# Splitting four V pages of a two-layer decode kernel into transfers of uneven row counts

## The chip, the core and the metric

The kernel runs on one core of a Trainium2 chip. The core has five engines with separate instruction streams: TensorE (PE) for matrix products, VectorE (DVE), ScalarE (ACT), GpSimd (POOL) and SyncE (SP), which here does nothing but issue transfers (DMAs) from the chip's main memory (HBM) to the on-chip memory of 128 partitions. The transfers are carried out by 16 DMA engines that work in parallel. The metric is the device time of one execution in microseconds (us). The kernel before takes 526.69 us, the median of two runs (526.36 and 527.03).

## The reference

Two layers, each of them an attention block and a gated feed-forward block, are applied to a single token of width 640. Both layers use the same weights and the same cache of keys and values.

```python
def _A_ref(x, k_cache, v_cache, wq, wo):      # Hq = Hkv = 32 heads, Dh = 192, Sk = 32768
    W = min(4096, max(256, Sk // 4))          # 4096: only the last 4096 positions count
    q = (x @ wq).reshape(B, Sq, Hq, Dh)       # (transposed to heads first)
    k = k_cache[:, :, Sk - W:, :]
    v = v_cache[:, :, Sk - W:, :]
    p = softmax(einsum("bhqd,bhkd->bhqk", q, k) * Dh ** -0.5)
    return einsum("bhqk,bhkd->bhqd", p, v).reshape(B, Sq, Hq * Dh) @ wo

def _B_ref(x, w1, w3, w2):                    # width 640 -> 1536 -> 640
    return (silu(x @ w1) * (x @ w3)) @ w2

x = x + _A_ref(layernorm(x), ...);  x = x + _B_ref(layernorm(x), ...)   # layer 0
x = x + _A_ref(layernorm(x), ...);  x = x + _B_ref(layernorm(x), ...)   # layer 1
```

One head's keys of the window are 4096 x 192 numbers of two bytes, 1.5 MB, and so are its values. For 32 heads and two layers that is most of what the kernel has to read.

## The kernel before

**Pages.** The keys or the values of one head are a page: 128 partitions x 6144 elements (`PGW`), that is 128 rows of 12,288 bytes, one row to a partition. The pages lie in one large tile, `arena`, of 32 units (`NUNIT`) of half a page each. Sixteen pages fit at once. The weights (wq, wo, w1, w3, w2) pass through the same units in pieces.

**The list of loads.** Before any work is recorded, a loop over the layers (lines 192 to 235) fills the list `loads`. An entry is a key, the number of units, and a list of parts; a part is an offset within the page's row, a width and a source in HBM. A whole page has one part:

```python
src = cache[0, h, S0:SK, :].rearrange("(p t) d -> p (t d)", p=P)
...
    loads.append(((kind, layer, h), 2, [(0, PGW, src)]))
```

In layer 0 the entries are: wq in three pieces, then K pages and V pages alternately, with V running `LEAD` = 6 heads behind K, then wo and the feed-forward weights. Layer 1 reads V again, and K for the heads that were not kept in `arena` from layer 0 (`RETAIN`).

**Issue.** `refill` takes the head of the list as long as `place` finds free units for it, and records one transfer on SP's queue for each part:

```python
for off, w, src in parts:
    pin(nc.sync.dma_start(out=arena[:, s * U + off:s * U + off + w], in_=src))
```

`done` frees a page's units after its last use and calls `refill`. So the order of the transfers is that of the list, and a transfer waits until whatever used its units before is done. There is a second wait, which the program's own list of waits shows: the completion of transfers is counted on eight semaphores in turn, and each transfer waits until the one eight places before it has landed completely. At most eight transfers are under way at a time. SP works strictly in order.

**Use of a page.** `k_page` (line 379 and the matrix products behind it) turns a K page by two DVE transposes and multiplies it with the queries; `softmax_head` and `softmax_place` turn four heads' scores into weights; `v_page` multiplies them with a V page, which must have landed whole. All matrix products are recorded by the helper `mm` (line 86). `combine`, `wo_proj` and `ffn` end a layer.

Of the kernel before, what the change touches and what calls it, by code (L numbers as in the profile page):

```python
# [15 lines left out]
P = 128  # L16
# [9 lines left out]
PGW = 6144  # L26
# [3 lines left out]
U = PGW // 2  # L30
# [8 lines left out]
MW = 2 * HB  # L39
PW = MW * HB  # L40
SPLIT = (("k", 12),)
KW = 4 * HB
WH = 6 * KW + 32 - KW
KEEP = 2400
# [3 lines left out]
def _ap(t, p0, npart, off, dims):  # L48
    ps = t.ap[0][0]
    return bass.AP(t.tensor, t.offset + p0 * ps + off, [[ps, npart]] + [list(d) for d in dims])  # L50
# [3 lines left out]
def kernel(  # L54
# [13 lines left out]
    nc = tc.nc  # L68
# [12 lines left out]
    def pin(ins):  # L81
        tc.keep_in_program_order(ins)
        return ins

    def mm(*a, **k):
        return pin(nc.tensor.matmul(*a, **k))  # L86
# [58 lines left out]
    arena = arn.tile([P, NUNIT * U], BF16, name="arena")  # L145
# [7 lines left out]
    loads = []  # L153
# [9 lines left out]
    def head(layer, g):  # L163
        return HG * ORDER[layer][g // HG] + g % HG

    def k_head(layer, g):
        return HG * ORDER[1][0] + (0, 1, 2, 3, 6, 4, 5, 7)[g] if layer == 1 and g < HG else head(layer, g)

    def k_first(layer, i):
        return layer == 0 and H - HB <= i < H  # L170

    def wo_units(layer):
        if layer == 0:
            return [(("o", 0, 0), [(1, 0, 2880)]), (("o", 0, 1), [(1, 2880, 5760)]), (None, [(0, 0, 5120), (1, 6720, 7680)]),
                    (("o", 0, 2), [(1, 5760, 6720), (2, 0, 1920)]), (("o", 0, 3), [(2, 1920, 4800)]),
                    (("o", 0, 4), [(2, 4800, 7680)]), (("o", 0, 5), [(3, 0, 2880)]), (("o", 0, 6), [(3, 2880, 5760)]),
                    (("o", 0, 7), [(3, 5760, 7680)]), (None, [(0, 5120, 7680)])]
        return [(("o", 1, 0), [(0, 0, 7680)]), (("o", 1, 1), [(1, 0, 7680)]), (("o", 1, 2), [(2, 0, 6720)])]
# [4 lines left out]
    def q_pieces(layer):  # L183
        if layer == 0:
            at = (0, 12, 24, 60)
            return [tuple(range(a, b)) for a, b in zip(at, at[1:])]
        return [tuple(range(12 * c + 6 * f, 12 * c + 6 * f + 6)) for f in range(2) for c in range(NCH)]

    def units_of(width):
        return -(-width // U)  # L190

    for layer in range(2):
        for piece in q_pieces(layer):
            n, at = 512 * len(piece), 512 * piece[0]
            loads.append((("q", layer, piece[0]), units_of(n), [(0, n, wq_r[:, at:at + n])]))
        for i in range(H + LEAD):
            kinds = (("v", i - LEAD, A_v_cache), ("k", i, A_k_cache))
            for kind, g, cache in kinds[::-1] if k_first(layer, i) else kinds:
                if not 0 <= g < H:
                    continue  # L200
                h = k_head(layer, g) if kind == "k" else head(layer, g)
                if kind == "k" and layer == 1 and h in RETAIN:
                    if h == STASH:
                        loads.append((("k", 1, h), 2, []))
                    continue
                src = cache[0, h, S0:SK, :].rearrange("(p t) d -> p (t d)", p=P)
                if layer == 1 and (kind, h) in SPLIT:
                    for th in range(2):
                        loads.append(((kind, layer, h, th), 1, [(0, U, src[:, U * th:U * th + U])]))
                else:  # L210
                    loads.append(((kind, layer, h), 2, [(0, PGW, src)]))
        for key, ranges in wo_units(layer):
            at, parts = 0, []
            for pos, lo, hi in ranges:
                parts.append((at, hi - lo, wo_v[ORDER[layer][pos]][:, lo:hi]))
                at += hi - lo
            if key:
                loads.append((key, units_of(at), parts))
            else:
                dst = wo5 if at == 2560 else wo4  # L220
                loads.append((None, None if dst is wo5 else LAST, [(dst[:, o:o + n], src) for o, n, src in parts]))
        if layer == 0:
            loads.append((("fa", layer), 1, [(0, 3072, w1_v[:, 0:3072])]))
            loads.append((("fb", layer), 1, [(0, 3072, w1_v[:, 3072:6144])]))
            loads.append((("fc", layer), 1, [(0, 1536, w1_v[:, 6144:]), (1536, 1536, w3_v[:, 0:1536])]))
            loads.append((("fd", layer), 1, [(0, 3072, w3_v[:, 1536:4608])]))
            loads.append((("fe", layer), 1, [(0, 3072, w3_v[:, 4608:])]))
            loads.append((("fg", layer), 1, [(0, W2A, w2_v[:, 0:W2A])]))
            loads.append((("fh", layer), 1, [(0, 7680 - KEEP - W2A, w2_v[:, W2A:7680 - KEEP])]))
            loads.append((None, None, [(keep[:], w2_v[:, 7680 - KEEP:7680])]))  # L230
        else:
            loads.append((("fa", layer), units_of(7680), [(0, 7680, w1_v[:, 0:7680])]))
            loads.append((("fb", layer), 2, [(0, PGW, w3_v[:, 0:PGW])]))
            loads.append((("fc", layer), 1, [(0, 1536, w3_v[:, PGW:])]))
            loads.append((("fd", layer), 2, [(o, n, w2_v[:, o:o + n]) for o, n in ((0, 3200), (3200, 1280), (4480, 3200 - KEEP))]))

    def place(key, n):
        at = [s for s in free if all(s + i in free for i in range(n))]
        if n == 2:
            at = [s for s in at if s % 2 == 0] or at  # L240
        kind, layer, x = (key + (None,))[:3]
        if layer == 0 and kind == "k" and x in RETAIN and x != STASH:
            return min((s for s in at if s < LAST), default=None)
        if layer == 0 and kind == "o":
            at = [s for s in at if s < LAST]
        if n == 1:
            return min(at, key=lambda s: (s ^ 1) in free, default=None)
        return max(at, default=None)

    def refill():  # L250
        while loads:
            key, n, parts = loads[0]
            if key is None:
                if n is not None:
                    if n not in free or n + 1 not in free:
                        return
                    free.remove(n)
                    free.remove(n + 1)
                for dst, src in parts:
                    pin(nc.sync.dma_start(out=dst, in_=src))  # L260
                loads.pop(0)
                continue
            s = place(key, n)
            if s is None:
                return
            home[key] = list(range(s, s + n))
            for i in home[key]:
                free.remove(i)
            loads.pop(0)
            for off, w, src in parts:  # L270
                pin(nc.sync.dma_start(out=arena[:, s * U + off:s * U + off + w], in_=src))  # L271
            if not parts:
                stash(arena[:, s * U:s * U + PGW], False)

    def stash(x, save):
        xu, pu, ru = x.bitcast(U32), pss[:].bitcast(U32), rest[:].bitcast(U32)
        at = 0
        for t, lo, n in [(pu, 512 * k, 512) for k in range(5)] + [(pu, MB + MN, 512 - MN), (ru, 0, MN)]:
            a, p = xu[:, at:at + n], t[:, lo:lo + n]
            pin(nc.vector.tensor_copy(out=p if save else a, in_=a if save else p))  # L280
            at += n
# [76 lines left out]
    def build_w(layer, b, first):  # L358
        engs = (nc.gpsimd, nc.scalar) + ((nc.vector, nc.vector) if first else (nc.gpsimd, nc.scalar))
        for a in range(4):  # L360
            dst = _ap(wst[:], 32 * a, 32, KW // 4 * a + HB - 1, [[WH - 1, HB], [KW, 6]])
            src = _ap(qt_sb[:], 0 if first else 32 * a, 32, 6 * HB * b, [[6, HB], [1, 6]])
# [18 lines left out]
    def k_page(layer, g, s_ps):  # L381
# [4 lines left out]
        for n in range(6):  # L386
            it = 5 - n
            be, par = divmod(it, 2)
            first = g % HB == 0 and n == 0
            w = 32 if first else KW  # L390
            for th in range(2):
                mm(s_ps[32 * th:32 * th + w, :], lhsT=wst[:, hl, KW * it:KW * it + w],
                   rhs=_ap(half(key, th), 0, P, 64 * be + par, [[192, 16], [2, 32]]),
# [7 lines left out]
    def softmax_head(b, s_ps):  # L401
# [7 lines left out]
        mb = _ap(m8[:], 0, 32, 0, [[0, 4], [1, HB]])  # L409
        pin(nc.vector.tensor_scalar_mul(out=tb[0:32, 0:KW].rearrange("p (a z) -> p a z", a=4), in0=mb, scalar1=-SCALE))  # L410
        pin(nc.scalar.mul(out=tb[32:64, 0:KW].rearrange("p (a z) -> p a z", a=4), in_=mb, mul=-SCALE))  # L411
        pin(nc.vector.transpose(nbt[:], tb[:]))  # L412
# [278 lines left out]
```

## Time and profile before

| what | value |
|---|---|
| median of two runs | 526.69 us |
| the profiled execution's own time | 525.68 us |
| its span | 523.7 us |
| PE, DVE, ACT, POOL busy | 286.0, 255.8, 66.0, 19.1 us |
| bytes moved by DMA | 220.12 MB, 420 GB/s over the span |
| transfers of whole K and V pages | 49 + 64, 1536 KB each |

The profile is a record of one execution. "Busy" is the time in which an engine worked on an instruction; for the DMA engines the share is a mean over all 16. The chain of waits is followed back from the last instruction: at each step it names what the instruction waited for last. A wait of SP's queue (SPq) says what a transfer waited for before it was issued. The record also holds each single packet that a DMA engine moved, with its size and duration but without the number of its engine, and for each transfer the marks that its engines set when their shares have landed.

### The profile page before, as it was taken

The numbers are of one execution on the slowest core, as the hardware profiler recorded it, in microseconds if no ns is written. First come the engines' busy times: TensorE is split into PE (matmuls) and PEld (weight loads), VectorE is DVE, ScalarE is ACT, GpSimd is POOL, SyncE is SP. The second block draws the span as 40 slices with busy tenths as digits, with TensorE's granted clock in tenths as the row PEclk, the third lists the DMA queues.
The fourth block names the chain that finished last, engine by engine and source line by source line (L and its number), as shares of the span: only waits on it lengthen the run. The fifth ranks groups of instructions, "written<-read, shape, count | busy, mean of one in ns | idle before, by whom it ended". The sixth has DMA issues, their size and how long they took to land.

```text
span 523.7 us, 5996 instructions
## 1 busy us (share of the span) xinstructions
PE 286.0 (55%) x2396; PEld 111.3 (21%) x2396; DVE 255.8 (49%) x385; ACT 66.0 (13%) x202; POOL 19.1 (4%) x86
## 2 busy tenths in 40 slices
PE   3335555463655544655555685676356565365564
PEld 1101222121222111212112231232112222122132
DVE  0079885656746476763002117431678565565002
ACT  1010210110202020202001022121201120112000
POOL 4010000000000000000000001000000000001000
PEclk9967778675776768666555577788557867776567
DMA  9999999999999999999999999999999999999996
GB/s 376 406 432 428 428 431 428 429 429 429 429 430 428 431 429 427 430 429 429 424 420 403 388 412 433 428 426 431 426 432 430 426 432 426 431 431 427 431 428 251
DMA packets 22931, 220.12 MB, mean 420 GB/s; under 512 B 2680, under 2 KB 3064, under 8 KB 7288
## 3 DMA queue, kind: packets, MB, share of 16 engines
q1 hardware_dynamic: 22760, 219.75, 99.2%
q8 instruction: 19, 0.31, 0.2%
q14 instruction: 8, 0.07, 0.0%
q10 hardware_dynamic: 144, 0.00, 0.0%
HBM read 219.74 MB, written 0.00 MB: 420 GB/s over the span
## 4 chain that ended last, share of the span: by engine, by line
DMA 84%; PE 10%; DVE 3%; issue 1%; ACT 1%; SPq 1%; DVEq 0%; ACTq 0%
DMA arena<-in_A_k_cache_dram 47%; DMA arena<-in_A_v_cache_dram 24%; DMA arena<-in_B_w_dram 6%; PE s_ps L86 5%; PE o_ps L86 2%; DVE arena L379 2%; DMA arena<-in_A_wo_dram 2%; DMA keep<-in_B_w_dram 2%; DMA arena<-in_A_wq_dram 1%; DMA wo<-in_A_wo_dram 1%; PE q_ps L86 1%; PE pss L86 1%; SPq L271 1%; PE u_ps L86 0%; PE y_ps L86 0%
## 5 line engine op out<-in xcount | busy, mean ns | idle before, releaser
L86 PE MATMUL s_ps<-arena,wst 128*16 128x512 bf16 (+1 forms) x768 | 157.7, 524 | 157.4 <-DVE arena L379 80.7
L379 DVE STREAM_TRANSPOSE arena<-arena 128x1536 uint32<-128x1536 uint32 x100 | 171.1, 1753 | 67.0 <-DMA arena<-in_A_k_cache_dram 66.5
L86 PE MATMUL o_ps<-arena,ptm 128*8 128x384 bf16 (+1 forms) x1024 | 115.2, 438 | 24.0 <-DMA arena<-in_A_v_cache_dram 24.0
L86 PEld LDWEIGHTS <-wst 128*16 128x16 bf16 (+1 forms) x768 | 48.9, 108 | 248.3 <-issue 216.1
L86 PEld LDWEIGHTS <-ptm 128*8 128x8 bf16 (+1 forms) x1030 | 40.7, 102 | 65.1 <-issue 53.4
L411 ACT ACTIVATE nt<-m 32x16 f32<-32x16 f32 x16 | 3.4, 213 | 271.4 <-DVE m L408 271.4
L427 ACT COPY ptm<-w 32x64 bf16<-32x64 bf16 x80 | 23.6, 295 | 46.5 <-PE o_ps L86 44.2
L86 PE MATMUL q_ps<-arena,xs 128*32 128x512 bf16 x120 | 19.2, 589 | 13.4 <-DMA arena<-in_A_wq_dram 12.3
L363 POOL COPY wst<-qt_sb 32x24 bf16<-32x24 bf16 x30 | 8.4, 280 | 422.9 <-PE s_ps L86 307.1
L459 DVE SCALAR_TENSOR_TENSOR w<-pss,sc,cb 64x192 bf16<-64x192 f32 x16 | 6.7, 416 | 33.5 <-PE pss L86 33.5
L402 DVE TENSOR_REDUCE lt<-s_ps 64x1 f32<-64x512 f32 x16 | 10.9, 684 | 23.0 <-PE s_ps L86 22.6
L86 PE MATMUL y_ps<-arena,otd 128*1 128x320 bf16 x176 | 15.3, 438 | 9.8 <-DMA arena<-in_A_wo_dram 9.3
L417 DVE STREAM_TRANSPOSE w<-w 64x512 bf16<-64x512 bf16 x16 | 11.3, 705 | 14.4 <-ACT w L414 14.4
L312 DVE CAST w<-y_ps 128x320 bf16<-128x320 f32 x3 | 1.5, 491 | 30.6 <-PE y_ps L86 30.6
L350 DVE CAST qt_sb<-pss 32x48 bf16<-32x48 f32 (+1 forms) x4 | 1.2, 307 | 28.6 <-ACT qt_sb L350 28.6
L86 PEld LDWEIGHTS <-xs 128*32 128x32 bf16 x200 | 8.3, 114 | 32.0 <-issue 25.2
L427 DVE COPY ptm<-w 32x64 bf16<-32x64 bf16 x48 | 10.0, 209 | 10.0 <-PE o_ps L86 8.9
L432 DVE RECIPROCAL sc<-pss 64x1 f32<-64x1 f32 x16 | 2.6, 165 | 23.1 <-PE pss L86 22.9
L452 ACT CAST w<-o_ps 128x384 bf16<-128x384 f32 x16 | 7.7, 479 | 31.8 <-PE o_ps L86 24.9
L414 ACT ACTIVATE w<-s_ps,nt 64x512 bf16<-64x512 f32 x16 | 10.9, 682 | 5.7 <-DVE nt L412 5.7
L86 PE MATMUL pss<-w,sel 128*64 128x192 bf16 x32 | 6.3, 286 | 8.1 <-ACT w L452 5.1
L86 PEld LDWEIGHTS <-otd 128*1 128x1 bf16 x192 | 5.8, 102 | 20.3 <-issue 15.8
(81 smaller groups left out, 119.2 us busy)
## 6 DMA issues: line engine op xcount, KB each, us to landing
arena<-in_A_v_cache_dram SPq DMA_DIRECT2D x64, 1536.0 KB, 29.2
arena<-in_A_k_cache_dram SPq DMA_DIRECT2D x49, 1536.0 KB, 29.2
arena<-in_A_wq_dram SPq DMA_DIRECT2D x10, 768.0 KB, 6.7
arena<-in_A_wq_dram SPq DMA_DIRECT2D x1, 4608.0 KB, 20.0
arena<-in_A_wo_dram SPq DMA_DIRECT2D x6, 720.0 KB, 8.7
arena<-in_A_wo_dram SPq DMA_DIRECT2D x2, 1920.0 KB, 30.1
arena<-in_A_wq_dram SPq DMA_DIRECT2D x2, 1536.0 KB, 7.7
arena<-in_B_w_dram SPq DMA_DIRECT2D x4, 768.0 KB, 7.1
```

What stands on the lines that cost most here:

```text
L86: return pin(nc.tensor.matmul(*a, **k))
L271: pin(nc.sync.dma_start(out=arena[:, s * U + off:s * U + off + w], in_=src))
L363: pin((engs[a].copy if engs[a] is nc.scalar else engs[a].tensor_copy)(out=dst, in_=src))
L379: pin(nc.vector.transpose(x, x))
L402: pin(nc.vector.reduce_max(out=t0[:, 0:1], in_=s_ps[0:64, :], axis=AX.X))
L411: pin(nc.scalar.mul(out=tb[32:64, 0:KW].rearrange("p (a z) -> p a z", a=4), in_=mb, mul=-SCALE))
L414: pin(nc.scalar.activation(out=e[:], in_=s_ps[0:64, :], func=ACTF.Exp, bias=nbt[:, 0:1], scale=SCALE, accum_out=l[0:64]))
L417: pin(nc.vector.transpose(et[:], e[:]))
L427: pin((eng.copy if eng is nc.scalar else eng.tensor_copy)(out=dst, in_=src))
L432: pin(nc.vector.reciprocal(out=rl[half], in_=rl_ps[half]))
L452: pin(nc.scalar.copy(out=o_sb[:, 0:384], in_=o_ps[:, 0:384]))
L459: pin(nc.vector.scalar_tensor_tensor(out=om, in0=ot_ps[half], scalar=rl[half], in1=mask[half].unsqueeze(2).broadcast_to([64, 16, 12]), op0 ...
```

## The change

For four of the 32 V pages of layer 0, those of the heads at places g = 0, 2, 4 and 6 of the order, the one part of 128 rows becomes several parts that lie one below the other: each covers the full width of the page, and a range of its rows and partitions. A part now carries its first row as a fourth field. The new table's name is `ROWS`.

```diff
+ROWS = {0: (80, 15, 14, 13, 6), 2: (80, 12, 11, 10, 9, 6), 4: (96, 8, 7, 6, 5, 4, 2), 6: (112, 12, 3, 1)}
...
-                    loads.append(((kind, layer, h), 2, [(0, PGW, src)]))
+                    parts, p0 = [], 0
+                    for n in ROWS.get(g, (P,)) if kind == "v" and layer == 0 else (P,):
+                        parts.append((0, PGW, src[p0:p0 + n], p0))
+                        p0 += n
+                    loads.append(((kind, layer, h), 2, parts))
...
-            for off, w, src in parts:
-                pin(nc.sync.dma_start(out=arena[:, s * U + off:s * U + off + w], in_=src))
+            for off, w, src, *at in parts:
+                p0 = at[0] if at else 0
+                pin(nc.sync.dma_start(out=arena[p0:p0 + src.shape[0], s * U + off:s * U + off + w], in_=src))
```

The four pages take 5, 6, 7 and 4 transfers instead of one each: 18 more on SP's queue. The bytes, their sources and their places in `arena` are the same. The order of the instructions on PE, DVE, ACT and POOL is the same too; only the semaphores that some of them wait for are others, and the first product with a split page waits for all of its parts. The four pages are the 7th, 11th, 15th and 19th K or V page that is loaded; in the record of before their last rows land between 48 and 93 us.

## The prediction

> **What bounds the kernel now.** I read the page first: are the DMA engines ever idle?
>
> ```profile
> DMA  9999999999999999999999999999999999999996
> GB/s 376 406 432 428 428 431 428 429 429 429 429 430 428 431 429 427 430 429 429 424 420 403 388 412 433 428 426 431 426 432 430 426 432 426 431 431 427 431 428 251
> ...
> q1 hardware_dynamic: 22760, 219.75, 99.2%
> ...
> DMA 84%; PE 10%; DVE 3%; issue 1%; ACT 1%; SPq 1%; DVEq 0%; ACTq 0%
> ...
> arena<-in_A_v_cache_dram SPq DMA_DIRECT2D x64, 1536.0 KB, 29.2
> arena<-in_A_k_cache_dram SPq DMA_DIRECT2D x49, 1536.0 KB, 29.2
> ```
>
> All 16 DMA engines are busy for 99.2% of the span, and DMA holds 84% of the chain that ended last. A page takes 29.2 us from issue to landing. SP's timeline from 20 us on shows how often one comes:
>
> ```profile
> 25.29 0.33 SPq L271 DMA_DIRECT2D arena<-in_A_v_cache_dram  x1
> 28.91 0.33 SPq L271 DMA_DIRECT2D arena<-in_A_k_cache_dram  x1
> 32.55 0.33 SPq L271 DMA_DIRECT2D arena<-in_A_v_cache_dram  x1
> 36.24 0.33 SPq L271 DMA_DIRECT2D arena<-in_A_k_cache_dram  x1
> ```
>
> One in 3.65 us, so eight are queued at any time (29.2 / 3.65). SP's waits say what releases each, summed, counted and the longest:
>
> ```profile
> SPq L271 <- DMA arena<-in_A_v_cache_dram: 191.2, 58, 7.1
> SPq L271 <- DMA arena<-in_A_k_cache_dram: 133.9, 42, 3.4
> ```
>
> A transfer waits for an earlier one to land, not for compute. The stretch between the layers is the only place before the tail where the DMA share falls (columns: stretch, length, busy PE, PEld, DVE, ACT, POOL, clock, DMA share, GB/s):
>
> ```profile
> 282.00:285.00 3.00, 0.86 (x11) 0.53 (x12) 0.57 (x3) 0.18 (x1) 0.00 (x0) 0.50 0.96 374
> 294.00:297.00 3.00, 2.55 (x18) 0.95 (x19) 0.61 (x4) 0.41 (x2) 0.00 (x0) 0.50 0.96 363
> 297.00:300.00 3.00, 1.42 (x8) 0.28 (x6) 0.00 (x0) 0.00 (x0) 0.00 (x0) 0.50 0.92 340
> ```
>
> That is 3 x (0.04 + 0.04 + 0.08) = 0.5 us of idleness per engine. So the time is the work of the DMA engine that finishes last. What I need is each engine's own load.
>
> **Two facts from the single packets and landing marks.** A 12,288-byte row is one packet of 460 ns, a 36,864-byte one 1364 ns: 24,576 bytes in 904 ns, 27.2 bytes per ns, on every engine and nearly without variation. An 8 KB packet of instructions, which goes to another memory, takes 309 ns: the same rate. So a row occupies its engine for 0.456 us (3.65 / 8). And the 16 marks of a page lie 1.75 to 2.0 us apart from 55 to 257 us, in nearly the same pattern from page to page: an engine that is late does not catch up. At the end the last engine trails the first by 2.80 us at 516.2 and still by 2.72 us at 520.3, though the others run out of work. So one engine's idleness does not speed up another; a row too many on one costs 0.456 us.
>
> **Part 1, rows per engine (on the path).** Before, each engine has 8 of a page's 128 rows. The final output, four rows, leaves five marks instead of 16: four rows, four engines, and one mark for the rest. I take it that n rows go to the largest number of engines, at most 16, that divides n: 80, 96 and 112 rows to all (5, 6, 7 each), the small parts to n engines with one row each. Which n, no row of before shows. One end is always the same first ones, the other that the places move round. I choose the first, since a transfer has nothing else to start from. [...] Then engine 0 gets 9 + 10 + 12 + 10 = 41 rows instead of 32, engine 1 40, engine 5 36, engine 7 32, engine 15 5 + 5 + 6 + 7 = 23. The heaviest has 9 more: 9 x 0.456 = **+4.1 us**.
>
> **Part 2, more transfers.** Engine 0 takes part in 22 transfers where it took part in 4. A page costs an engine 3.645 us, of which 8 x 12,288 / 27.2 = 3.614 is data; 0.03 us is left for the completion mark and the change of transfer. 18 x 0.03 = **+0.5 us** (0 to 0.5).
>
> **Part 3, who was late anyway.** Only the amount by which engine 0 overtakes the former last engine counts. In the page that landed at 253.3 us the 16 marks trail the last by 1.9 (first) to 0, on average 0.9. Engine 0's place among them is not shown: **-0.9 us** (-1.9 to 0).
>
> **Part 4, SP's queue.** 18 more issues at 0.33 us are 5.9 us in a queue that waited 325 us for landings: 0. If it could not wait, 5.9 us would be the price.
>
> **Part 5, fewer bytes under way.** Each part takes one of the eight places. The worst is page g = 4: its seven parts and the K page behind them fill all eight, so that K page goes out only when the K page ahead of them has landed, and an engine then has nothing left but its share of page 4: 6 rows, 2.7 us, for the light ones, 12 rows for engine 0. The first transfer was issued at 0.74 us and its first packet began at 1.75: 1.0 us. So the rings stay filled, by 1.7 us for the light ones; should they run dry, it strikes the engines that are ahead. 0. Behind a waiting issue on SP's queue stand only later loads, with at least two pages (7 us) queued in the rings again after page 6.
>
> **Part 6, consumers.** A split page's first product waits for several marks, and each V page lands up to 4 us later; they are a consequence of part 1, not added. The dry 0.5 us between the layers may absorb something (-0.5 to 0; I take 0, as a later landing moves the chain there with it).
>
> Sum: 4.1 + 0.5 - 0.9 = +3.7 us, from 4.1 - 1.9 - 0.5 = +1.7 to +4.6. On the profiled execution's 525.68 us that is 529.4; the median lies 1.0 higher, so **530.4 us** (528.4 to 531.3), 0.7% slower.
>
> **Rivals.**
>
> *B, the small parts do not run side by side.* In every transfer of before engine and partitions are paired in the same way, 8 rows each, so nothing shows what happens when several engines write neighbouring partitions at once. A part of n rows costs an engine in it between 0.456 us (side by side) and n x 0.456 (in turn). All 18 parts: 18 x 0.456 = 8.2 us to 144 rows x 0.456 = 65.7. For it speaks that the only measured rate, 27.2 bytes per ns, may be that of the engine or of the entry that it always writes to; against it, that instructions, which go elsewhere, move at the same rate, so the engine by itself explains it. Priced at three in turn, it adds 2 x 8.2 = 16.4: 530.4 + 16.4 = **546.8 us** (two: 538.6; four: 555.0). It decides beyond 2% from 1.8 in turn on ((10.5 - 3.7) / 8.2 = 0.83 more). [...]
>
> *C, not slower: the load comes out even.* If the places of the small parts move round the engines, each gets about 32 rows again and part 1 is gone. What is left is part 2 spread thin (144 / 16 + 4 = 13 transfers per engine instead of 4: 9 x 0.03 = +0.3). If the extra rows also happen to miss the engines that trail, the last one could move to the mean: the 16 marks at 516.2 us trail by 1.6 on average, -1.6. So 525.1 to 527.2, say **526.4 us**. Against it: nothing in the instruction could make the place move. It decides as soon as the heaviest engine has no more than 2 rows too many (2 x 0.456 = 0.9, the lead).
>
> *D, the small parts go to one engine each, or wholly in turn.* 144 rows on one engine, and 23 from the large parts: 167 instead of 32, 135 x 0.456 = +61.6: **588 us**. Against it speak the output's four rows with four marks.
>
> **How the numbers follow.** Chances: the forecast 0.47, B 0.36, C 0.12, D 0.05. The range reaches from the better half of C to B in fours short of its end: 525.8 to 551, which leaves out 0.05 below and some 0.13 above. The forecast alone: 528.4 to 531.3. Two per cent is 10.5 us, about what a measurement of this kernel can tell from no change. Faster by so much: no case reaches 516, 0.02 for what I do not see. Within: the forecast, C, and the low end of B, 0.60. Slower: the rest of B and D, 0.38.
>
> **What would show it.** In the profile of the changed kernel: small parts' packets of 12,288 bytes at 460 ns (the forecast), or at two to four times that (B); n marks from n rows, plus one for the rest; after page 6 the marks of a whole page 6 to 9 us apart instead of 1.8, since engine 15 has 18 rows less than engine 0 (18 x 0.456 = 8.2), and still so at 200 us (C: under 3); SP's waits still on landings, none of them longer than 10 us; DMA share below 0.99 in the slices after 90 us only by what light engines lose. The forecast fails if packets stretch, if the marks close up again before the end without the time growing, or if the stretch between the layers (255 to 310 us) turns the 4 us into more by running dry.

## The result and the profile after

The changed kernel takes 557.34 us (two runs, 557.11 and 557.56) against 526.69: a ratio of 1.058, with an interval of 1.056 to 1.061. It is 5.8% slower. The profiled execution took 557.56 us, 555.8 of them span. The forecast of 530.4 us is missed, and so is the upper end of the range, 551.

The page of the changed kernel, its lines that answer to those of before (slices of the span, 13.9 us each; the queue; the shares of the chain; the transfers of whole pages, with KB each and the median us to landing):

```profile
DMA  8999998999999999999999999999999999999995
GB/s 357 432 428 250 328 289 222 347 280 430 431 428 428 430 428 430 429 430 428 409 410 404 394 351 409 430 427 429 428 428 429 429 431 429 430 427 432 430 430 231
...
q1 hardware_dynamic: 22904, 219.75, 98.5%
...
DMA 82%; PE 10%; DVE 5%; ACT 1%; issue 1%; SPq 0%; DVEq 0%; ACTq 0%
...
arena<-in_A_v_cache_dram SPq DMA_DIRECT2D x60, 1536.0 KB, 29.2
arena<-in_A_k_cache_dram SPq DMA_DIRECT2D x49, 1536.0 KB, 24.4
```

DMA still holds 82% of the chain, and the engines still count as busy, 98.5% of the span. The queue has 144 packets more than before (22,904 against 22,760), as many as the small parts have rows: one mark more for each. But in six slices, the fourth to the ninth, the rate falls from 430 to between 222 and 347 GB/s. Those are the 40 to 125 us in which the four cut pages come. The shortfall of the six against 430 is 864 GB/s in all; times 13.9 us and divided by 430 this is 27.9 us of transfer at full rate, most of the 31 us. A queue that is busy while its bytes come at half the rate has no gaps: its packets have become longer.

Stretches of 4 us show where (stretch, length, busy PE, PEld, DVE, ACT, POOL, clock, DMA share, GB/s; a packet is counted whole where it begins, so a share can exceed 1):

```profile
44.00:48.00 4.00, 3.10 (x20) 1.05 (x18) 4.00 (x3) 0.00 (x0) 0.00 (x0) 0.78 1.13 222
48.00:52.00 4.00, 0.62 (x5) 0.09 (x1) 3.75 (x7) 0.01 (x1) 0.56 (x2) 1.00 0.95 123
...
88.00:92.00 4.00, 3.29 (x26) 1.38 (x28) 0.71 (x1) 0.58 (x2) 0.00 (x0) 0.50 0.68 151
...
108.00:112.00 4.00, 3.09 (x27) 1.10 (x21) 0.00 (x0) 0.00 (x0) 0.00 (x0) 0.68 1.03 230
...
124.00:128.00 4.00, 0.00 (x0) 0.00 (x0) 2.16 (x2) 0.00 (x0) 0.00 (x0) 0.53 1.01 430
```

The first two hold V page 0: its 80-row part, then its small parts. The share stays near 1, and the rate is 222 and then 123 GB/s. The third holds mainly the 96-row part of page 4: here the share falls to 0.68, so some rings (an engine's list of rows still to move) are empty. With 0.86 and 0.92 in the next two stretches this is 4 x (0.32 + 0.14 + 0.08) = 2.2 us of idleness, on average over the 16 engines, which was not there before. The fourth holds little else than the 112-row part of page 6: 230 GB/s. The last one lies behind all cut pages, at the old rate.

The single packets say the same. Before, 14,802 of 14,848 rows of 12,288 bytes took 0.46 us. In the stretch of the 112-row part 74 of 75 rows took 0.8 to 1.0 us. In that of the small parts of page 0, 35 of 40 took 1.3 to 1.9 us. From 124 to 128 us all 140 took 0.46 us again.

SP's waits (summed, counted, longest) are still mostly for landings:

```profile
SPq L277 <- DMA arena<-in_A_v_cache_dram: 201.5, 71, 6.7
SPq L277 <- DMA arena<-in_A_k_cache_dram: 138.3, 41, 7.0
```

Two single waits for DVE, of 3.3 us each and behind 130 us, are new; otherwise the releasers are those of before, and no wait for a page is longer than 7.0 us. The longest of them lies ahead of the empty rings, in SP's timeline (start, duration, transfers):

```profile
72.87 0.33 SPq L277 DMA_DIRECT2D arena<-in_A_k_cache_dram  x1
74.26 11.37 SPq L277 DMA_DIRECT2D arena<-in_A_v_cache_dram  x7
92.62 0.35 SPq L277 DMA_DIRECT2D arena<-in_A_k_cache_dram  x1
```

The seven parts of page 4 are out by 85.6 us and fill all eight places with the K page ahead of them; the K page behind them goes out at 92.6, when that one has landed. Its 16 marks lie 8.5 us apart, so that engines which were done with it at 84 us had nothing but their six rows of the 96-row part and one or another small row.

### The profile page after: what moved, and what is told of

The parts are those of the page before. It is cut to its first block, busy times and chain, and to the rows that moved or that the text cites. A ratio compares the mean times of both kernels' runs of the same rounds, so it can differ in the third digit from the quotient of the medians.

```text
span 555.8 us, 6026 instructions
## 1 busy us (share of the span) xinstructions
PE 291.4 (52%) x2396; PEld 110.8 (20%) x2396; DVE 256.2 (46%) x385; ACT 66.0 (12%) x202; POOL 19.2 (3%) x86
## 3 DMA queue, kind: packets, MB, share of 16 engines
q1 hardware_dynamic: 22904, 219.75, 98.5%
## 4 chain that ended last, share of the span: by engine, by line
DMA 82%; PE 10%; DVE 5%; ACT 1%; issue 1%; SPq 0%; DVEq 0%; ACTq 0%
DMA arena<-in_A_k_cache_dram 38%; DMA arena<-in_A_v_cache_dram 30%; DMA arena<-in_B_w_dram 7%; PE s_ps L87 5%; DVE arena L385 3%; DMA arena<-in_A_wq_dram 2%; PE o_ps L87 2%; DMA arena<-in_A_wo_dram 2%; DMA wo<-in_A_wo_dram 1%; DMA xb<-in_A_x_dram 1%; PE pss L87 1%; PE q_ps L87 1%; PE y_ps L87 1%; PE u_ps L87 1%; ACT ptm L433 1%
## 5 line engine op out<-in xcount | busy, mean ns | idle before, releaser
L87 PE MATMUL s_ps<-arena,wst 128*16 128x512 bf16 (+1 forms) x768 | 163.0, 538 | 174.2 <-DVE arena L385 94.1
L87 PE MATMUL q_ps<-arena,xs 128*32 128x512 bf16 x120 | 17.3, 548 | 14.2 <-DMA arena<-in_A_wq_dram 13.0
L433 DVE COPY ptm<-w 32x64 bf16<-32x64 bf16 x48 | 10.0, 208 | 10.5 <-PE o_ps L87 9.4
```

The lines of the kernel that those rows point to most:

```text
L433: pin((eng.copy if eng is nc.scalar else eng.tensor_copy)(out=dst, in_=src))
```

## The experiments

Two theories stood against each other, and a third beside them. **S**: a part of fewer than 128 rows deals its rows to the DMA engines so that several of them write behind the same entry of the arena's memory at once (an entry is whatever a group of partitions shares when it is written; the word belongs to the theory). Each row then takes two to four times as long, in the large parts too, and whole pages that pass at the same time are slowed. **U**: what counts is the most loaded engine's number of rows, as the forecast said. **N**: the number of transfers costs, through SP's queue, the places for transfers under way, or an engine's change of transfer. The expectations of two runs name a fourth, **O**: a row off its engine's usual partitions runs at half rate, wherever it lies. In the kernels e1 to f4 the table's entries are (first row, rows, step), and the loops of the change pass the step on; h1 and h2 cut columns in place of rows; h3 and h4 are the changed kernel with a shorter table. Times of before in the same jobs were 526.1 to 526.3 us.

A landing below is the last mark of a page in the trace; the table gives by how many us it came later than in the profile of before. The K page that follows each cut V page is taken.

| K page behind | changed | e1_multiples | f1_sixteens | h3_page4 | h4_page0 |
|---|---|---|---|---|---|
| V page 0 | 5.8 | 4.2 | 4.4 | -0.1 | 5.7 |
| V page 2 | 15.0 | 9.0 | 9.9 | -0.1 | 5.7 |
| V page 4 | 22.6 | 13.6 | 14.7 | 7.9 | 6.1 |
| V page 6 | 29.9 | 18.7 | 18.9 | 7.9 | 6.1 |

### Even load, few transfers

```diff
-ROWS = {0: (80, 15, 14, 13, 6), 2: (80, 12, 11, 10, 9, 6), 4: (96, 8, 7, 6, 5, 4, 2), 6: (112, 12, 3, 1)}
+ROWS = {g: ((0, a, 1), (a, P - a, 1)) for g, a in ((0, 80), (2, 80), (4, 96), (6, 112))}
```

> The four pages come in two parts each, 80 + 48, 80 + 48, 96 + 32 and 112 + 16 rows: all numbers of rows are multiples of 16, so every engine has 8 rows of each page, and only 4 transfers are added. Theory S (entries are shared): when the rows of a part are dealt to the engines so that several of them write neighbouring partitions at once, their packets stretch; the record of the changed kernel shows all packets of the 112-row part at 0.86 to 0.9 us instead of 0.46. Then this kernel costs at least 4 x 3.65 = 14.6 us (every row of four pages at twice its duration), 541 to 552 us in all. Theory U (uneven load: the engine with the most rows sets the time): about no change, 526.7 + 4 x 0.03 = 527 us. Theory N (the number of transfers, and fewer bytes under way): 4/18 of the 30.6 us, 533 to 534 us.

Measured: 545.48 us, ratio 1.034 (1.031 to 1.038). All parts have a multiple of 16 rows, so by part 1 each engine has its 8 rows of a page (in the changed kernel parts of 80, 96 and 112 rows set 16 marks), and there are only four more transfers. Still some 60% of the loss is there, so U alone can't be the cause. Stretches of this kernel around page 4 and page 6 (columns as above):

```profile
84.00:88.00 4.00, 3.15 (x25) 1.11 (x22) 3.38 (x2) 1.47 (x5) 0.00 (x0) 0.58 1.03 214
...
100.00:104.00 4.00, 2.47 (x21) 0.85 (x15) 0.00 (x0) 0.00 (x0) 0.00 (x0) 0.50 1.02 233
...
112.00:116.00 4.00, 0.08 (x4) 0.00 (x0) 1.40 (x1) 0.00 (x0) 0.00 (x0) 0.83 1.02 436
```

While the large parts pass, the rate is 214 and 233 GB/s with the share above 1; it is 436 as soon as whole pages pass alone. The mean row takes 0.85 to 0.97 us in such stretches; eight rows an engine at 0.9 instead of 0.46 us are 3.5 us a page. The landings show 4.2 to 5.1 us a page; at least a part of the rest lies in the neighbours (below).

### The same number of transfers, cut by columns

```diff
+COLS = {0: 2, 2: 2, 4: 2, 6: 2}                  # h1_columns2
+COLS = {0: 5, 2: 6, 4: 7, 6: 4}                  # h2_columns_many
...
+                    for j in range(n):
+                        lo, hi = PGW * j // n // 32 * 32, PGW * (j + 1) // n // 32 * 32
+                        parts.append((lo, hi - lo, src[:, lo:hi]))
```

> V pages 0, 2, 4 and 6 of layer 0 are cut in two again, as many transfers as in e1_multiples (4 more than before), but by columns: each transfer covers all 128 rows and half of their 12,288 bytes. Theory S (a transfer of fewer than 128 rows deals its rows to the DMA engines so that two or more of them write behind the same entry of the arena's memory): nothing is shared here, all packets keep their unshared length. Before, packets of 6,144 bytes took 234 ns at the median, 8 ns over two halves of 460: 8 rows on an engine and page, 0.06 us a page, 0.3 us in all: 526.0 to 527.3 us. Rival N (the number of transfers costs, whatever their shape; e1's 18.9 us would be 4.7 us for each added transfer): 545 us.

> The same four pages in 5, 6, 7 and 4 transfers, as many as in the changed kernel (18 more than before), cut by columns: 128 rows each, 1,728 to 3,072 bytes of a row. It leaves the count of transfers, SP's queue, the eight places of transfers under way and their fewer bytes as in the changed kernel, and takes away the cut by rows, the uneven load and the sharing. By the packets of before (2,560 bytes 102 ns, 1,920 bytes 79, 3,072 bytes 121, against 460 for 12,288) a row costs some 30, 40, 60 and 24 ns more: 8 rows an engine, 1.2 us over the four pages. Theory S: 526.8 to 529 us. Rival N (the count, or too few bytes under way, makes a good part of the 30.7 us): over 535 us.

Measured: h1_columns2 526.07 us, ratio 0.9996 (0.998 to 1.001); h2_columns_many 527.57 us, ratio 1.003 (1.002 to 1.004). The page of the first (slices):

```profile
DMA  9999999999999999999999999999999999999996
GB/s 370 409 432 428 425 428 427 431 429 428 428 431 428 429 433 425 429 431 428 423 422 403 395 382 432 427 427 430 428 429 429 431 428 430 430 427 431 431 429 252
```

And of the second:

```profile
DMA  9999999999999999999999999999999999999995
GB/s 375 406 430 424 423 415 425 430 432 430 423 432 432 426 429 433 430 424 430 425 419 407 394 410 431 430 427 426 432 430 423 432 432 429 427 432 430 430 426 223
```

No slice between 40 and 125 us falls below 415 GB/s. h1 has as many transfers as e1, in the same places of the queue, and its 19 us are gone: what costs is the cut by rows. h2 has exactly the 18 added transfers of the changed kernel, its queue, its eight places and, page for page, its bytes under way. It adds 1.7 us (1.1 to 2.3 by the interval), of which the shorter packets were expected to make 1.2. In its trace the K page behind V page 6 lands 0.9 us late. N falls, for 29 of the 31 us.

### One cut page alone

```diff
+ROWS = {4: (96, 8, 7, 6, 5, 4, 2)}               # h3_page4
+ROWS = {0: (80, 15, 14, 13, 6)}                  # h4_page0
```

> Only V page 4 of layer 0 is cut as in the changed kernel (96, 8, 7, 6, 5, 4, 2 rows); pages 0, 2 and 6 are whole. Theory S (each cut page has its own price in rows that are written at a half to a quarter of the speed, its neighbours' included; in the changed kernel K page 9 and this page added 7.7 us, from 15.2 to 23.0): 533 to 536 us. Theory A (what counts is the rows of the most loaded engine: 6 + 6 = 12 in place of 8, four times 0.46 = 1.8 us): 527.5 to 529 us. If the pages' prices do not add up (a loss that comes from rings that run dry only after several cut pages): under 532 us.

> Only V page 0 of layer 0 is cut as in the changed kernel (80, 15, 14, 13, 6 rows); pages 2, 4 and 6 are whole. Theory S: the 5.8 us by which this page landed later in the changed kernel, and nothing after it: 531.3 to 533.5 us. Theory A: the most loaded engine has 5 + 4 = 9 rows in place of 8, 0.46 us: 526.3 to 527.5 us.

Measured: h3_page4 535.43 us, ratio 1.017 (1.015 to 1.019); h4_page0 531.36 us, ratio 1.010 (1.008 to 1.012). The page of the first (slices of 13.3 us):

```profile
GB/s 369 412 429 431 433 299 323 429 433 431 427 429 429 426 432 431 430 428 412 418 403 379 407 404 429 429 428 431 426 429 428 430 432 428 429 427 430 432 427 230
```

And of the second (13.2 us):

```profile
GB/s 372 411 430 244 422 430 428 431 428 430 426 430 431 426 431 428 431 429 429 423 418 410 416 402 413 429 427 430 426 429 430 429 430 428 430 429 431 431 426 256
```

One dent for one page, and the full rate on both sides of it. Page 4 alone lands 7.9 us late where it and its neighbour added 7.6 in the changed kernel; page 0 alone 5.7 against 5.8. So these two pages have a price of their own, whatever is cut beside them; pages 2 and 6 were not cut alone. U's 1.8 and 0.5 us (theory A in the expectations) are far off.

h3 also answers what the empty rings cost. Its stretches around page 4:

```profile
72.00:76.00 4.00, 1.88 (x14) 0.77 (x16) 1.70 (x4) 1.57 (x5) 0.00 (x0) 0.50 1.11 276
76.00:80.00 4.00, 3.67 (x31) 1.24 (x24) 3.44 (x5) 1.87 (x6) 0.00 (x0) 0.66 0.98 163
80.00:84.00 4.00, 0.94 (x7) 0.32 (x4) 1.07 (x3) 0.08 (x1) 0.00 (x0) 1.00 1.09 169
84.00:88.00 4.00, 1.47 (x16) 0.53 (x16) 0.00 (x0) 0.00 (x0) 0.00 (x0) 0.70 0.89 338
88.00:92.00 4.00, 0.58 (x1) 0.17 (x2) 2.69 (x2) 0.00 (x0) 0.00 (x0) 0.50 0.99 421
```

The shares are 1.01 on average, so no ring ran empty here, and the page costs 7.9 us. In the changed kernel, with the 2.2 us of idleness, it costs 7.6. The empty rings added nothing there that the last mark shows.

The neighbours show too. In h3 the whole K page ahead of V page 4 lands 1.5 us late, although nothing is issued differently before it; its other 15 marks come at most 0.7 us late. The reading, argued and not tried by itself: an engine that has finished its share of that page goes on to the cut part, and its rows there slow those of engines that still have some of that page to move.

### Small parts of 16 rows, and rows further apart

```diff
+ROWS = {g: ((0, a, 1),) + tuple((b, 16, 1) for b in range(a, P, 16))
+        for g, a in ((0, 80), (2, 80), (4, 96), (6, 112))}                    # f1_sixteens
+ROWS = {g: ((0, a, 1),) + tuple((a + j, 16, (P - a) // 16) for j in range((P - a) // 16))
+        for g, a in ((0, 80), (2, 80), (4, 96), (6, 112))}                    # f2_sixteens_apart
+ROWS = {g: tuple((j, 16, 7) for j in range(7)) + ((112, 16, 1),) for g in (0, 2, 4, 6)}  # e2_apart7
+ROWS = {g: tuple((j, 16, 8) for j in range(8)) for g in (0, 2, 4, 6)}         # e3_apart8
```

> The large parts as in the changed kernel (80, 80, 96, 112 rows), and the rest of each page in parts of 16 neighbouring rows: 3, 3, 2 and 1 of them, so 9 transfers more than before, and 8 rows per engine and page. The kernel with the rest in one part (4 transfers more) took 545.5 us. Theory S, sharing of entries alone: how a rest of 48 rows is cut changes nothing, 545.5 to 547 us. Theory N, the number of transfers (the 11 us between 545.5 and the changed kernel's 557.3 go with its 14 further transfers): 545.5 + 5/14 x 11.8 = 549.7 us. Theory U, uneven load makes those 11 us: 545.5 us.

> As the kernel with parts of 16 neighbouring rows, the same transfers and the same load, but the rows of the 16-row parts lie 3 apart where there are three such parts, and 2 apart where there are two. [...] Theory S: faster than with neighbours, by up to 0.9 us for each of 8 parts, 538.5 to 545 us; if the engines have already fallen out of step, so that they take turns at the entries, by less. Theories N and U: no difference.

> The four pages come in eight parts of 16 rows each, 28 transfers more than before; the rows of seven of the parts lie 7 partitions apart (j, j + 7, ... j + 105), those of the eighth are 112 to 127. Load is even. [...] Theory O (an engine that writes to partitions other than its usual ones does so at half rate): every row at 0.9, +3.65 a page, 541 us or more, as much as with rows 8 apart. Theory N (number of transfers): more than the changed kernel, 28/18 of 30.6 us = +47, 574 us. Theory U: 527 to 528 us.

> As the kernel with rows 7 apart, but eight parts of 16 rows that lie 8 partitions apart (j, j + 8, ... j + 120). The number of transfers, the rows per engine and the bytes under way are the same in both. [...] Theories O, N and U: the same as with rows 7 apart (541, 574 and 527 us).

Measured: f1_sixteens 546.72 us, ratio 1.039 (1.037 to 1.040); f2_sixteens_apart 551.67, 1.049 (1.046 to 1.051); e2_apart7 558.28, 1.061 (1.059 to 1.063); e3_apart8 562.52, 1.069 (1.067 to 1.071). f2 lies 6.7 us above the upper end of what S expected of it, and no run shows the 0.9 us a part by which it was to be faster than f1: it is 5.0 us slower. e2 and e3 are slower still. But in the transfers up to 70 us the distance of the rows does tell. In f1 the stretches of the small parts of pages 0 and 2:

```profile
48.00:52.00 4.00, 0.59 (x5) 0.07 (x1) 3.75 (x8) 0.03 (x1) 0.56 (x2) 1.00 0.87 151
...
68.00:72.00 4.00, 1.51 (x11) 0.48 (x10) 0.16 (x1) 0.00 (x0) 0.56 (x2) 1.00 0.93 166
```

The first 4 us of the cut page 0 in e2_apart7, whose 16 rows lie 7 apart:

```profile
44.00:48.00 4.00, 0.00 (x0) 0.00 (x0) 0.00 (x0) 0.00 (x0) 0.00 (x0) 0.50 1.06 280
```

And in e3_apart8, 8 apart (that no engine computes in either is told below):

```profile
44.00:48.00 4.00, 0.00 (x0) 0.00 (x0) 0.00 (x0) 0.00 (x0) 0.00 (x0) 0.50 1.04 224
```

By part 1 each of these parts gives one row to each of 16 engines; the distance of the rows differs (and f1's lie in the upper part of the page alone). The mean row took 1.39 us among neighbours, 0.87 to 0.93 at a distance of 8, and 0.70 at 7. The rates, 151 to 166, 224 and 280 GB/s, are what some 6, 8 and 10 of the 16 engines would move at the 27.2 bytes per ns of before, as an estimate. After three cut pages (behind V page 4) e2 was 8.0 us late, e3 10.5, f2 11.4 and f1 14.7. So the rows' places decide how long a row takes, and theory O, which expected the same time at distances of 7 and 8, falls. Why 7 is faster than 8 was not tried, and these stretches hold rows of several parts at once.

What then made f2, e2 and e3 slow is another thing. DVE's timeline of f2_sixteens_apart (start, duration, what, and in brackets the idle time before it and what ended it):

```profile
89.52 3.44 DVE L386 STREAM_TRANSPOSE arena<-arena 128x1536 uint32<-128x1536 uint32 x2 [59.78 <-DMA arena<-in_A_v_cache_dram]
```

And SP's wait behind it, between 70 and 115 us:

```profile
SPq L278 <- DVE rest L287: 26.3, 1, 26.3
```

This is the first transpose of a K page, one that landed at 25 us. It waits, 60 us long, for the parts of the V pages: in f1 this instruction waits for one DMA semaphore, in f2 for five. The program has this instruction wait for transfers to every third row of other places of the arena too, so compute was held back, and at 70 us the loads found no free place. That wait is in the program, for the sake of the step, and is no property of the chip. The totals of these three say nothing of S; their transfers up to 70 us do.

### Only the lower half of the rows

```diff
+ROWS = {g: tuple((32 * a + o, 8, 4) for a in range(2) for o in range(4)) for g in (16, 18, 20, 22)}
```

> All pages come whole as in the kernel before, except that of four later V pages (g = 16, 18, 20, 22 of layer 0) only partitions 0 to 63 are loaded, in eight parts of eight rows that lie 4 partitions apart; the upper half of these pages is left out, and the products use what lies there. The 8 rows of a part go to 8 engines, one each, so eight engines have 8 rows per page as before and the other eight have none: 3 MB less in all. If the engine with the most rows sets the time, and idle engines do not speed up the others, the time stays at that of before but for the marks of 28 more transfers (28 x 0.03 = 0.8) and the lead of the eight (up to -1.6): 525 to 528 us. If a limit shared by all engines set the pace, 3.1 MB / 430 GB/s = 7.3 us would be saved: 519 to 520 us.

Measured: 572.54 us, ratio 1.087 (1.085 to 1.090), although rows 64 to 127 of four pages are left out. The rows took 0.46 us, as in a whole page (eight rows, 4 apart), but in each of these pages the engines ran dry, as its stretches show:

```profile
188.00:192.00 4.00, 2.81 (x22) 1.08 (x24) 2.88 (x2) 0.00 (x0) 0.00 (x0) 0.50 0.02 4
192.00:196.00 4.00, 3.74 (x34) 1.68 (x32) 1.49 (x6) 1.96 (x6) 0.00 (x0) 0.75 0.00 0
```

Its DVE at that point:

```profile
189.12 3.44 DVE L386 STREAM_TRANSPOSE arena<-arena 128x1536 uint32<-128x1536 uint32 x2 [10.14 <-DMA arena<-in_A_v_cache_dram]
```

The same step-made waits: the transpose of a K page waits 10 us for V parts, and SP waits up to 10.8 us for products of PE before it may load on. The run was to bound what idle engines cost; it doesn't. h2, above, answers the question of the bytes under way without steps. Of e4 only the packets count: 0.46 us for rows 4 apart, 1.3 us for neighbours in the next runs.

### Parts of eight rows, on two pages

```diff
+ROWS = {g: ((0, 80, 1),) + tuple((80 + 8 * j, 8, 1) for j in range(6)) for g in (0, 2)}   # f3_eights
+ROWS = {g: ((0, 80, 1),) + tuple((80 + j, 8, 6) for j in range(6)) for g in (0, 2)}       # f4_eights_apart
```

> Only the pages g = 0 and 2 are split: 80 rows, then six parts of 8 neighbouring rows. Eight engines get 5 + 6 = 11 rows of such a page, the other eight 5; 12 transfers are added. Theory U (rows of the fullest engine): 2 pages x 3 rows x 0.456 = 2.7 us, plus what the 80-row parts cost by themselves (in the kernel of multiples the first two split pages cost 4.2 and 4.8 us), so 529 to 538 us. [...] Theory N: 12/18 x 30.6 = 20 us, 547 us, as much as with rows 6 apart.

In f4 the eight rows of a small part lie 6 partitions apart; the transfers and the uneven load are those of f3:

> [...] Theory S: the rows of the small parts take 0.46 to 0.6 us again, and only the 80-row parts and the uneven load are left: 531 to 540 us, 10 us or more below the kernel with neighbours. Theory U and theory N: no difference between the two.

Measured: f3_eights 545.36 us, ratio 1.037 (1.035 to 1.039); f4_eights_apart 544.24, 1.034 (1.030 to 1.038). f3 cuts only two pages and costs as much as e1 with four. Behind V page 2 it is 17.8 us late, f1 with the same 80 rows and an even load 9.9. The difference is 7.9 us for six rows (11 instead of 8 on eight engines, twice): **1.3 us for each row too many**, which is what these rows take (on average 1.33 us in page 0 and 1.27 in page 2). It is a mean: page 0 adds 3.5 us for its three rows and page 2 adds 4.4 (there some rings were empty, with DMA shares of 0.92 and 0.69 from 64 to 72 us). f4 misses S's expectation: no run shows the 0.6 us of a row that it allows for, and its rows, 6 apart, still took 1.2 to 1.3 us. All 48 rows of the small parts lie in the upper half, and the eight engines without a row in them were on the whole pages ahead and behind, which have rows there too. That this is why is argued from the packets, not tested. (Its rows have a step too, and DVE's first transpose of a K page, which waits for eight DMA semaphores, stood for 49.6 us; the landings behind V page 2 stay 15 to 16.6 us late, so hardly a load was held back by it.) Taken alone, f3 and f4 would also suit theory N, which expected 547 us for f3 and the same for f4; it is h2 that rules N out.

## Why the prediction was wrong

**What bounds the kernel** was right: the end goes with the transfers, and the chain and SP's waits are mostly of the same kind after the change. So was the rule of **part 1** for the number of engines: the marks in the trace are 16 for parts of 80, 96 and 112 rows, and n and one more for parts of n rows, in every transfer. Rival D falls with that. For numbers of rows that no kernel here has, the rule is the author's estimate. Rival C falls by the marks of later whole pages: they are 4.65 us apart where C expected under 3. In f3 the marks of the K page behind V page 0 come in two groups, eight from 56.5 to 57.0 us and eight from 59.1 to 59.9, as when the parts of eight rows go to the same eight engines each time.

**The step that failed** is the price of a row in part 1: 0.456 us, read from whole pages, was taken for the rows of every part. Only rival B doubted it, with the sentence "A part of n rows costs an engine in it between 0.456 us (side by side) and n x 0.456 (in turn)", and only for the 18 small parts; the rows of the large parts stand in the sum at 0.456 us without a reason. The runs showed in its place:
- *No term for the large parts.* A row of a part with all 16 engines in it takes longer too: 0.88 us. With their multiples of 16 rows and the slowed neighbours, cuts with an even load cost 18.7 to 18.9 us (e1, f1). The sum had nothing there.
- *Part 1 mis-sized.* The nine rows too many were priced at 0.456 us, 4.1 us. The changed kernel lies 11.0 us behind f1 (29.9 - 18.9), 1.2 us a row; f3 measured 1.3. By pages the difference is 1.4, 3.7, 2.7 and 3.2 us for 1, 2, 4 and 2 rows too many, so the price per row holds for the sum and not page by page.

18.9 and 11.0 are the 29.9 us at page 6; the delay stays at 29.5 to 29.9 us for all later pages of layer 0, up to 287 us, and the medians are 30.7 us apart.

The reason given against B, that instructions "move at the same rate, so the engine by itself explains it", was no evidence. A packet of instructions says nothing of rows that several engines write side by side, and only those of 8 KB moved at that rate, 309 ns at the median; the 19 packets of 16 KB took 0.88 to 1.24 us, where 27.2 bytes per ns make 0.60. B was put up for the small parts alone; the 0.88 us of the 112-row part show that the large ones needed it too. B was right about the packets, given 0.36. Its price for small parts (three in turn, 546.8 us) was near what their packets show (1.3 to 1.5 us). That they run in fours (1.8 us), from which the upper end of the range was taken, no run shows; the large parts carried the time above it.

**Part 2** (+0.5 us): h2 measures 1.7 for as many transfers, 1.2 of it expected from shorter packets; what is left fits, though the interval of 1.1 to 2.3 can't tell it from nothing. **Part 3** (-0.9) can't be seen beside 30 us. **Part 4** (0) and **part 5** (0) stand by h2. In the changed kernel, though, the case that part 5 described for page 4 came true: it saw the light engines' rings "filled, by 1.7 us", and rings were empty for about 2 us an engine, on average, at 88 to 100 us. That it struck only engines that were ahead, as part 5 said, fits h3, where the page costs as much without it. The marks of the K page ahead were 8.5 us apart by then, and SP waits for the last of them. In h2, with its even load, the same queue does not run dry. **Part 6** (0) is nearly right. The last pages of layer 0 land 29.7 us late and the first of layer 1 31.4 us; the spans of the two profiled executions are 32.1 us apart. The stretch between the layers ran dry for 3 x (0.23 + 0.22) = 1.35 us, more than the 0.5 us of before:

```profile
324.00:327.00 3.00, 2.33 (x16) 1.48 (x17) 0.93 (x6) 0.41 (x2) 0.00 (x0) 0.50 0.77 307
327.00:330.00 3.00, 1.67 (x14) 0.42 (x12) 0.00 (x0) 0.00 (x0) 0.00 (x0) 0.66 0.78 238
```

That is one of the signs that the prediction named for its failing, but worth under 2 of the 31 us; whether the dry time made them was not tried.

Of the **signs** named, the packets told it at once. The 16 marks of a whole page lay 4.65 us apart from 150 to 268 us, as a sign of the uneven load, but less than the 6 to 9 us expected; which part of that the empty rings took back was not tried. From 349 to 459 us, behind the stretch between the layers, they were 1.6 to 1.9 us apart.

What stays open: which row goes to which engine in a part of fewer than 128 rows. The records name no engine. That all whole pages are dealt to the engines in the same way, as B has it, is read from their marks, 16 a page and some 1.7 to 2.0 us from first to last, in nearly the same pattern from page to page. Nor is it shown what makes the rows longer: an entry that several engines share is theory S's word for it, and since a row's place in the arena and its place in HBM go together in all these runs, they can't tell on which side it lies. And f4's rows, 6 apart, took 1.2 to 1.3 us against the theory's 0.46 to 0.6, for a reason that is only argued.

No run points to a version that is faster than before; cutting by columns is free at best.

## What to carry over

Where DMA engines bound a kernel, ask not only how many engines a transfer uses but how long its rows take on them: here a row of 12,288 bytes took 0.46 us in a whole page of 128 rows and 0.88 us in a part of 112 rows on as many engines. If a page has to come in several transfers, cut its columns and keep all 128 rows: for the four pages here that cost 1.7 us with 18 more transfers, against 19 us and more for cuts by rows. And when bytes per second fall while the busy share stays at its top, look at the length of single packets before looking for waits.

## What the runs showed that was not expected

- 16 busy engines can move 215 to 235 GB/s instead of 430, with a busy share of 1.0: the 112-row part (0.88 us a row) and the 80- and 96-row parts alike.
- A cut page came with a delay of the transfer ahead of it in the queue: the whole K page ahead of cut page 4 landed 1.5 us late, with no change before it (h3).
- The length of a row of 12,288 bytes goes with the step between the rows of its part: 0.46, 0.70, 0.87 to 0.93 and 1.39 us for steps of 4 (eight rows), 7, 8 and 1 (sixteen). A step of 6 (eight rows, in the upper part of the page) took 1.2 to 1.3 us.
- Twice as many transfers with half the columns cost nothing (0.9996); four to seven on a page cost 0.4 us a page.
